# A gate by reciprocal, one product moved between engines, and a new order of all steps in a fused attention and channel-mixing kernel

## The chip, the cores and the metric

The kernel runs on one core of one Trainium2 chip. The metric is device time in microseconds (us), and of several runs the median. The core's engines work side by side and meet through semaphores: TensorE (PE in the profile) multiplies matrices and writes to PSUM, VectorE (DVE), ScalarE (ACT) and GpSimd (POOL) work elementwise, SyncE (SP) issues the DMA transfers here. Each engine takes its own instructions strictly in the order in which they stand.

## The reference

For four batches, attention of 12288 queries of width 128 over 768 keys, which are also the values; then a channel-mixing block on the attention's output.

```python
kv_pool = kv.reshape(B, H // r, r, W // r, r, C).mean(axis=(2, 4))
k = v = kv_pool.reshape(B, -1, C) @ w_sr
s = scale * (q @ k.transpose(0, 2, 1))
a = np.exp(s - s.max(-1, keepdims=True))
a /= a.sum(-1, keepdims=True) + 1e-09
x = a @ v

xk = mu_k * x + (1.0 - mu_k) * x_prev      # x_prev: x one position earlier
xr = mu_r * x + (1.0 - mu_r) * x_prev
k = np.maximum(xk @ w_k, 0.0)              # 128 -> 1024
v = k * k @ w_v                            # 1024 -> 128
r = 1.0 / (1.0 + np.exp(-(xr @ w_r)))      # the gate
out = r * v
```

All of it is float32, with inputs scaled so that the exponent of the gate can be large. The kernel keeps the accuracy by splitting operands of the fast matmuls into a high and a low part.

## The kernel before

A tile is 512 queries; there are 96 tiles, 24 per batch. Everything lies transposed, with the 128 channels on the partitions, except the scores.

The steps of a tile have short names, which the tables of times use; the profile shows the tile that a step writes.

- `qf` loads the queries, `qh` (ScalarE) and `ql` (GpSimd) split them.
- For each quarter s of the tile: `S` on TensorE gives 128x768 scores in PSUM; `nm` on VectorE their negated maximum; `ex` on ScalarE the exponentials (tile `pe`) and their sums. For two quarters at once `rc` on VectorE makes the scaled reciprocals of the sums, a TENSOR_SCALAR and a RECIPROCAL over 128x2. `f1` on ScalarE writes the high half of the weights (tile `pp`) and `f2` on VectorE the low half, from `pe` and the high half, both in SBUF. `tt` transposes them by DMA.
- `AV` on TensorE sums weights times values into `px` in PSUM. `xek` and `xer` (ScalarE), `xk` and `xr` (VectorE) mix it with the position before, and `xck`, `xcr` (GpSimd) copy the column that the next tile needs. `xkh` and `xrh` (VectorE) round to float16, and `xkl`, `xrl` (GpSimd) take the rest.
- For each quarter f of the 1024 hidden channels: `ha` and `hb` on TensorE give `ph`, 128x1024 in PSUM; `r` on ScalarE the positive part (tile `rr`). The square is needed as a float16 high part `kh` and a bfloat16 rest `kl`. A string with a figure per quarter says how: for "1" VectorE multiplies `ph` by `rr` (tile `kk`), ScalarE squares `rr` to float16 (`kh`) and GpSimd subtracts (`kl`); for "2" ScalarE squares to float32 (`kk`), VectorE casts it (`kh`) and GpSimd subtracts; for "3" VectorE multiplies in place in PSUM (profile: `ph<-ph,rr`) and also subtracts.
- `va` and `vb` on TensorE sum `kh` and `kl` times the second weights into `pv`.
- The gate: `z` on TensorE; `E` and `th` on ScalarE are the exponential and the hyperbolic tangent of half; `T1`, `E1` and `g` on VectorE make the gate of them, and `o` on VectorE multiplies `pv` by it. `so` stores `o`.

Keys of the next batch are made beside the tiles: twelve tiles of each of the first three batches hold one `br` (VectorE, TENSOR_REDUCE into `acc`), and later tiles the rest of that batch's preparation.

The order on every engine comes from tables of numbers. Each step of tile i gets the number `WHEN[step] + 19.3 * i` (the first and the last tiles have tables of their own, `EARLY` and `LATE`, the preparation `PREP` and `ONCE`), a heap hands the steps out by it, and a wrapper keeps each engine's instructions in that order:

```python
plan.add(places[name] + base, name, fn, ("tile", i))
while self.heap:
    heapq.heappop(self.heap)[2]()
```

Through the wrapper nearly every instruction is recorded under line 37, so the profile is read by tiles. PSUM holds three buffers of 128x1024, taken in turn by `S` and `ph`, one of 128x512 for `px` and the gate's `pz`, and one for `pv`.

Of the kernel before, what the change touches and what calls it, by code (L numbers as in the profile page):

```python
# [23 lines left out]
K_SHIFT = 23  # L24
# [47 lines left out]
def tile_kernel(ctx, tc, qT, kv0, kvw, w_sr, mu_k, mu_r, w_k, w_v, w_r, outT):  # L72
# [35 lines left out]
    cz = const.tile([P, 2], F32, name="cz")  # L108
# [3 lines left out]
    for name, shape, dtype in (  # L112
# [5 lines left out]
        ("E", [P, T], F32), ("th", [P, T], F32), ("o", [P, T], F32),  # L118
# [3 lines left out]
        ("s4", [P, 4], F32), ("uz", [P, 2], F32), ("sc", [P, 1], F32),  # L122
# [48 lines left out]
    def weights(name, w, hi, lo, half, extra):  # L171
# [6 lines left out]
        def part(i, c0, c1):  # L178
# [29 lines left out]
            @once(f"wi_{key}")  # L208
            def _():
                st["ei", i] = take("th", name="ei", dtype=I32)[:, :d]  # L210
                dve.tensor_scalar(
                    st["ei", i], st["ef", i], least, 2.0 ** 23, op0=ALU.subtract, op1=ALU.mult
                )
# [89 lines left out]
    @once("cz")  # L303
    def _():
        amp = one("amp_wr")
        unit = 1.0 / (scale * X_TOP)
        dve.tensor_scalar_mul(cz[:, 0:1], amp, unit)
        dve.tensor_scalar_mul(cz[:, 1:2], amp, 0.5 * unit)

    @once("cv")  # L310
    def _():
        unit = 1.0 / (scale * X_TOP)
        k2 = one("k2")
        dve.tensor_scalar(
            k2, one("amp_wk"), one("amp_wk"), 0.5 * unit * unit * 2.0 ** (2 * K_SHIFT),
            op0=ALU.mult, op1=ALU.mult,
        )
        dve.tensor_tensor(out=cv, in0=k2, in1=one("amp_wv"), op=ALU.mult)
# [187 lines left out]
    def plan_tile(i, b, t):  # L506
# [35 lines left out]
        for s in range(NSUB):  # L542
# [18 lines left out]
            @at(f"ex{s}")  # L561
            def _(s=s):
                if f"sm{s & 2}" not in st:
                    new(f"sm{s & 2}")
                act.activation(
                    out=new(f"pe{s}"), in_=st[f"S{s}"][:, :K], func=AF.Exp,
                    bias=st[f"nm{s}"], scale=1.0, accum_out=st[f"sm{s & 2}"][:, s % 2:s % 2 + 1],
                )
# [51 lines left out]
        for x, k in (("k", 0), ("r", 2)):  # L620
# [23 lines left out]
            def _(x=x):  # L644
                dve.tensor_copy(out=new(f"x{x}h"), in_=st[f"x{x}"])
# [15 lines left out]
        def _():  # L661
            act.activation(out=new("E"), in_=st["pz"], func=AF.Exp, scale=bps[b][5][:, 0:1])

        @at("th")
        def _():
            act.activation(out=new("th"), in_=st["pz"], func=AF.Tanh, scale=bps[b][5][:, 1:2])

        @at("T1")
        def _():
            th = st["th"].bitcast(I32)  # L670
            dve.tensor_single_scalar(th, th, 0x7FFFFFFF, op=ALU.bitwise_and)

        @at("E1")
        def _():
            dve.tensor_scalar(st["E"], st["E"], 1.0, bps[b][6], op0=ALU.min, op1=ALU.mult)

        @at("g")
        def _():
            dve.scalar_tensor_tensor(
                out=st["E"], in0=st["th"], scalar=1.0, in1=st["E"], op0=ALU.add, op1=ALU.mult  # L680
            )
# [76 lines left out]
        def _():  # L758
            dve.tensor_tensor(out=new("o"), in0=st["pv"], in1=st["E"], op=ALU.mult)
# [12 lines left out]
    for i, (b, t) in enumerate(seq):  # L772
# [8 lines left out]
KV = '1123'  # L781
# [12 lines left out]
    "xer": 88.618, "xcr": 88.633, "xck": 89.308, "xk": 89.863, "xkh": 91.073, "xr": 91.42,  # L794
# [14 lines left out]
    "ksl": 103.908,  # L809
# [38 lines left out]
        "xek": 112.355, "xer": 112.393, "xk": 112.842, "xcr": 113.081, "xr": 113.28, "xrh": 114.174,  # L848
# [222 lines left out]
```

## Time and profile before

| | |
|---|---|
| median of 3 runs | 2064.28 us (2064.04 to 2065.26) |
| the profiled execution | 2064.17 us, its span 2062.3 us |
| granted TensorE clock | 0.992 |
| busy, share of the span: PE, PEld, DVE, ACT, POOL | 93%, 51%, 96%, 83%, 56% |
| HBM read and written | 52.63 MB, 25.17 MB |

A row of the timeline gives start, duration, engine, operation, tile written and tiles read, shapes, and in brackets how long the engine was idle before and for whom. An instruction on VectorE starts some 0.07 us before the recorded end of the one ahead, so costs are best read from one start to the next. A row that groups instructions gives minimum, median and maximum in ns, or the summed time in us and the mean in ns. A row of a window gives its bounds, its length, the busy time of PE, PEld, DVE, ACT and POOL with the number of instructions, the granted clock, the share of DMA time and GB/s.

### The profile page before, as it was taken

To read this page: it belongs to the slowest core of one execution; us is meant where nothing else is said; L and a number is where in the kernel's file an instruction comes from. 1 tells how busy PE (TensorE), PEld (TensorE's weight loads), DVE (VectorE), ACT (ScalarE), POOL (GpSimd) and SP (SyncE) were. 2 spreads that over 40 slices of the span, in tenths; PEclk is the share of its full clock that TensorE was granted. 3 is DMA by queue.
4 is the path that set the end of the run, shared out by engine and by line. 5 is a ranking of instruction groups with operands and counts; after the bars stand their busy time and mean duration, and the time that the engine had idled before them with its cause. 6 is when DMAs were issued, how large, how long until landed. Compare 5 with 4: busy or idle time off the path is not lost. (4 is left out here: it accounts for less than half of the span.)

```text
span 2062.3 us, 26955 instructions
## 1 busy us (share of the span) xinstructions
PE 1911.9 (93%) x9022; PEld 1043.0 (51%) x9022; DVE 1987.1 (96%) x2581; ACT 1705.2 (83%) x2432; POOL 1155.9 (56%) x784
## 2 busy tenths in 40 slices
PE   6698999999999999999999999998999999999998
PEld 4344455554555555555555555554555555555553
DVE  6999999999999999999999999999999999999998
ACT  3687888888888888888888888887888888888896
POOL 1255565555555656556555656655565565555556
PEclk9899999999999999999999999999999999999999
DMA  7545455464656564644546565545445546455552
GB/s 218 125 96 132 108 126 100 91 115 82 124 112 142 114 140 106 118 88 100 105 105 140 111 145 111 125 84 111 93 106 99 117 89 123 89 116 106 104 101 58
DMA packets 640521, 230.56 MB, mean 112 GB/s; under 512 B 606336, under 2 KB 608640, under 8 KB 640384
## 3 DMA queue, kind: packets, MB, share of 16 engines
q1 hardware_dynamic: 640384, 228.85, 52.7%
q8 instruction: 71, 1.16, 0.3%
q14 instruction: 66, 0.54, 0.1%
HBM read 52.63 MB, written 25.17 MB: 38 GB/s over the span
## 5 line engine op out<-in xcount | busy, mean ns | idle before, releaser
L37 POOL TENSOR_TENSOR kl<-kk,kh 128x1024 bf16<-128x1024 f32 x288 | 688.0, 2390 | 478.3 <-ACT kh L37 230.2
L37 DVE SCALAR_TENSOR_TENSOR pp<-pe,rc,pp 128x768 f16<-128x768 f32 x384 | 552.2, 1474 | 0.1
L37 ACT ACTIVATE pe<-S,nm 128x768 f32<-128x768 f32 x384 | 346.2, 902 | 243.7 <-DVE nm L37 243.0
L37 ACT ACTIVATE rr<-ph 128x1024 f32<-128x1024 f32 x384 | 390.7, 1018 | 18.1 <-PE ph L37 14.4
L37 PE MATMUL px<-pT,v 128*128 128x512 f16 x1728 | 391.3, 379 | 2.8 <-DVE xr L37 2.3
L37 DVE TENSOR_REDUCE nm<-S 128x1 f32<-128x768 f32 x384 | 362.4, 945 | 3.8 <-PE S L37 3.4
L37 ACT ACTIVATE pp<-pe,rc 128x768 f16<-128x768 f32 x384 | 347.9, 932 | 7.9 <-DVE rc L37 2.6
L37 PE MATMUL S<-ksh,ql 128*128 128x512 f32 (+1 forms) x768 | 320.7, 418 | 34.7 <-DVE kk L37 20.0
L37 ACT ACTIVATE kh<-rr 128x1024 f16<-128x1024 f32 x288 | 303.1, 1053 | 0.5
L37 PE MATMUL ph<-xkh,wkl 128*128 128x512 f16 x768 | 293.4, 382 | 3.9 <-DVE kl L37 1.6
L37 PE MATMUL pv<-kh,wvl 128*128 128x512 f16 x768 | 293.3, 382 | 1.8 <-DVE kh L37 1.1
L37 PE MATMUL pv<-kh,wvh 128*128 128x512 f16 x768 | 292.0, 380 | 0.0
L37 PE MATMUL ph<-xkh,wkh 128*128 128x512 f16 x768 | 291.5, 380 | 0.0
L37 PEld LDWEIGHTS <-v 128*128 128x128 f16 x1728 | 168.6, 98 | 205.3 <-issue 3.0
L37 PE MATMUL S<-ksl,qh 128*128 128x512 f32 (+1 forms) x768 | 261.7, 341 | 0.4 <-DVE ksl L37 0.4
L37 PE MATMUL S<-ksh,qh 128*128 128x512 f32 (+1 forms) x768 | 261.1, 340 | 0.0
L37 POOL TENSOR_TENSOR ql<-qf,qh 128x512 fp32r<-128x512 f32 x96 | 123.8, 1289 | 206.7 <-ACT qh L37 206.7
L37 DVE TENSOR_TENSOR kk<-ph,rr 128x1024 f32<-128x1024 f32 x192 | 232.8, 1213 | 3.4 <-ACT rr L37 2.0
L37 PEld LDWEIGHTS <-wkh 128*128 128x128 f16 x1536 | 150.8, 98 | 165.0 <-issue 5.1
L37 PE MATMUL ph<-xkl,wkh 128*128 128x512 f16 x768 | 227.9, 379 | 0.0
L37 PE MATMUL pv<-kl,wvb 128*128 128x512 bf16 x768 | 227.3, 379 | 0.2 <-DVE kl L37 0.2
L37 PEld LDWEIGHTS S<-ksh,ql 128*128 128x128 f32 x768 | 146.4, 191 | 98.0 <-DVE kk L37 25.9
(116 smaller groups left out, 2651.6 us busy)
## 6 DMA issues: line engine op xcount, KB each, us to landing
qf<-qT SPq DMA_DIRECT2D x96, 256.0 KB, 3.3
outT<-o SPq DMA_DIRECT2D x96, 256.0 KB, 3.8
kvt<-kvw SPq DMA_DIRECT2D x36, 512.0 KB, 4.5
pT<-pp SPq DMA_TRANSPOSE x384, 4.1
kva<-kv SPq DMA_DIRECT2D x8, 512.0 KB, 5.5
kvb<-kv SPq DMA_DIRECT2D x4, 512.0 KB, 7.4
raw<-moe_w_k SPq DMA_DIRECT2D x2, 512.0 KB, 7.9
raw<-moe_w_v SPq DMA_DIRECT2D x2, 512.0 KB, 4.1
```

Of the source, the lines that this page charges most:

```text
L37: return self.tc.keep_in_program_order(op(*args, **kwargs))
```

## The change

- The gate becomes `E` (the exponential, now of minus z), `D` (VectorE: the smaller of E and 2^126, plus 1) and `g` (VectorE: RECIPROCAL in place over 128x512). `th` and `T1` go. The factor that `E1` multiplied in moves to `o`, which becomes a SCALAR_TENSOR_TENSOR.
- The third quarter of the hidden channels changes from "2" to "1": its product goes from ScalarE to VectorE, its rounding from VectorE to ScalarE.
- Two switches are added (where `pe` lies, and which engine makes `xkh`, `xrh` and `D`) and left as they were: SBUF and VectorE.
- All tables of numbers are new, and so is the order on every engine.

The core of the diff; of the tables only a line each is shown:

```diff
+                if PE_AT[s] == "P":
+                    st[f"pe{s}"] = st[f"S{s}"][:, :K]
+                else:
+                    new(f"pe{s}")
...
         @at("E")
         def _():
-            act.activation(out=new("E"), in_=st["pz"], func=AF.Exp, scale=bps[b][5][:, 0:1])
-
-        @at("th")
-        def _():
-            act.activation(out=new("th"), in_=st["pz"], func=AF.Tanh, scale=bps[b][5][:, 1:2])
-
-        @at("T1")
-        def _():
-            th = st["th"].bitcast(I32)
-            dve.tensor_single_scalar(th, th, 0x7FFFFFFF, op=ALU.bitwise_and)
-
-        @at("E1")
-        def _():
-            dve.tensor_scalar(st["E"], st["E"], 1.0, bps[b][6], op0=ALU.min, op1=ALU.mult)
+            act.activation(out=new("E"), in_=st["pz"], func=AF.Exp, scale=bps[b][5])
+
+        @at("D")
+        def _():
+            if CAST["D"] == "A":
+                act.activation(out=st["E"], in_=st["E"], func=AF.Copy, bias=1.0)
+            else:
+                dve.tensor_scalar(st["E"], st["E"], 2.0 ** 126, 1.0, op0=ALU.min, op1=ALU.add)
 
         @at("g")
         def _():
-            dve.scalar_tensor_tensor(
-                out=st["E"], in0=st["th"], scalar=1.0, in1=st["E"], op0=ALU.add, op1=ALU.mult
-            )
+            dve.reciprocal(st["E"], st["E"])
...
         @at("o")
         def _():
-            dve.tensor_tensor(out=new("o"), in0=st["pv"], in1=st["E"], op=ALU.mult)
+            dve.scalar_tensor_tensor(
+                out=new("o"), in0=st["pv"], scalar=bps[b][6], in1=st["E"], op0=ALU.mult, op1=ALU.mult
+            )
...
-KV = '1123'
+PE_AT = 'SSSS'
+CAST = {'k': 'D', 'r': 'D', 'D': 'D'}
+KV = '1113'
...
 WHEN = {
-    "br": 1.952, "qf": 14.922, "qh": 25.48, "ql": 28.691, "S0": 48.421, "S1": 49.355, "nm0": 49.552,
+    "br": 2.435, "qf": 13.848, "qh": 17.857, "ql": 24.148, "S0": 42.876, "nm0": 46.617,
...
```

What the tables move, at three places of an ordinary tile in the middle of the run. First VectorE around the gate, before, from the second `rc` of a tile on (`th` is `T1`, the two `E` are `E1` and `g`):

```order
L37 TENSOR_SCALAR rc<-sm 128x2
L37 RECIPROCAL rc<-rc 128x2
L37 CAST xrh<-xr 128x512
L37 TENSOR_SCALAR th<-th 128x512
L37 TENSOR_REDUCE nm<-S 128x1
L37 TENSOR_SCALAR E<-E,sc 128x512
L37 SCALAR_TENSOR_TENSOR E<-th,E 128x512
L37 TENSOR_TENSOR o<-pv,E 128x512
L37 TENSOR_TENSOR kk<-ph,rr 128x1024
```

and now (the TENSOR_SCALAR on `E` is `D`, the RECIPROCAL on `E` is `g`):

```order
L37 TENSOR_SCALAR rc<-sm 128x2
L37 RECIPROCAL rc<-rc 128x2
L37 TENSOR_REDUCE nm<-S 128x1
L37 CAST xrh<-xr 128x512
L37 SCALAR_TENSOR_TENSOR pp<-pe,rc,pp 128x768
L37 TENSOR_SCALAR E<-E 128x512
L37 TENSOR_REDUCE nm<-S 128x1
L37 RECIPROCAL E<-E 128x512
L37 SCALAR_TENSOR_TENSOR pp<-pe,rc,pp 128x768
```

The four `pp` steps of a tile no longer stand as two pairs: two of them stand singly on both sides of the gate. Then VectorE from the first `rc` behind this on, before:

```order
L37 TENSOR_SCALAR rc<-sm 128x2
L37 RECIPROCAL rc<-rc 128x2
L37 SCALAR_TENSOR_TENSOR pp<-pe,rc,pp 128x768 x2
L37 TENSOR_TENSOR kk<-ph,rr 128x1024
L37 SCALAR_TENSOR_TENSOR pp<-pe,rc,pp 128x768 x2
L37 TENSOR_REDUCE nm<-S 128x1
L37 SCALAR_TENSOR_TENSOR xk<-px,s_90,xek 128x512
L37 CAST xkh<-xk 128x512
L37 SCALAR_TENSOR_TENSOR xr<-px,s_90,xer 128x512
```

and now:

```order
L37 TENSOR_SCALAR rc<-sm 128x2
L37 RECIPROCAL rc<-rc 128x2
L37 SCALAR_TENSOR_TENSOR o<-pv,sc,E 128x512
L37 TENSOR_TENSOR kk<-ph,rr 128x1024
L37 SCALAR_TENSOR_TENSOR pp<-pe,rc,pp 128x768 x2
L37 SCALAR_TENSOR_TENSOR xr<-px,s_90,xer 128x512
L37 SCALAR_TENSOR_TENSOR xk<-px,s_90,xek 128x512
L37 TENSOR_TENSOR kk<-ph,rr 128x1024
L37 TENSOR_REDUCE nm<-S 128x1
L37 CAST xkh<-xk 128x512
```

One pair of `pp` is left, behind `o` and a product, and with four PSUM readers behind it; a `br`, in a tile that has one, stands between `o` and the product. The last place is GpSimd, one tile's worth before:

```order
L37 TENSOR_TENSOR ql<-qf,qh 128x512
L37 TENSOR_TENSOR kl<-kk,kh 128x1024
L37 COPY xer<-xer 128x1
L37 COPY xek<-xek 128x1
L37 TENSOR_TENSOR kl<-kk,kh 128x1024
L37 TENSOR_TENSOR xkl<-xk,xkh 128x512
L37 TENSOR_TENSOR kl<-kk,kh 128x1024
L37 TENSOR_TENSOR xrl<-xr,xrh 128x512
```

and now:

```order
L37 TENSOR_TENSOR ql<-qf,qh 128x512
L37 TENSOR_TENSOR kl<-kk,kh 128x1024 x2
L37 COPY xer<-xer 128x1
L37 TENSOR_TENSOR xkl<-xk,xkh 128x512
L37 TENSOR_TENSOR kl<-kk,kh 128x1024
L37 COPY xek<-xek 128x1
L37 TENSOR_TENSOR xrl<-xr,xrh 128x512
```

The first two `kl` of a tile now stand back to back behind `ql`, and the copies apart.

More of the change, by code (lines that the diff above doesn't have):

```diff
@@ L107, in tile_kernel @@
     mtop = const.tile([P, 2], F32, name="mtop")
-    cz = const.tile([P, 2], F32, name="cz")
+    cz = const.tile([P, 1], F32, name="cz")
     cv = const.tile([P, 1], F32, name="cv")
@@ L117, in tile_kernel @@
         ("xkh", [P, T], F16), ("xkl", [P, T], F16), ("xrh", [P, T], F16), ("xrl", [P, T], F16),
-        ("E", [P, T], F32), ("th", [P, T], F32), ("o", [P, T], F32),
+        ("E", [P, T], F32), ("ei", [P, T], F32), ("o", [P, T], F32),
         ("rr", [P, 2 * T], F32), ("kk", [P, 2 * T], F32), ("kh", [P, 2 * T], F16),
@@ L121, in tile_kernel @@
         ("ksh", [P, K], F32R), ("ksl", [P, K], F32R), ("v1", [P, NK, P], F16), ("v2", [P, NK, P], F16),
-        ("s4", [P, 4], F32), ("uz", [P, 2], F32), ("sc", [P, 1], F32),
+        ("s4", [P, 4], F32), ("uz", [P, 1], F32), ("sc", [P, 1], F32),
         ("ks", [P, K], F32), ("acc", [P, K], F32), ("dg", [P, 2, P], F32),
@@ L209, in _ @@
             def _():
-                st["ei", i] = take("th", name="ei", dtype=I32)[:, :d]
+                st["ei", i] = take("ei", dtype=I32)[:, :d]
                 dve.tensor_scalar(
@@ L306, in _ @@
         unit = 1.0 / (scale * X_TOP)
-        dve.tensor_scalar_mul(cz[:, 0:1], amp, unit)
-        dve.tensor_scalar_mul(cz[:, 1:2], amp, 0.5 * unit)
+        dve.tensor_scalar_mul(cz, amp, -unit)
     @once("cv")
@@ L314, in _ @@
         dve.tensor_scalar(
-            k2, one("amp_wk"), one("amp_wk"), 0.5 * unit * unit * 2.0 ** (2 * K_SHIFT),
+            k2, one("amp_wk"), one("amp_wk"), unit * unit * 2.0 ** (2 * K_SHIFT),
             op0=ALU.mult, op1=ALU.mult,
@@ L564, in _ @@
                     new(f"sm{s & 2}")
+                if PE_AT[s] == "P":
+                    st[f"pe{s}"] = st[f"S{s}"][:, :K]
+                else:
+                    new(f"pe{s}")
                 act.activation(
-                    out=new(f"pe{s}"), in_=st[f"S{s}"][:, :K], func=AF.Exp,
+                    out=st[f"pe{s}"], in_=st[f"S{s}"][:, :K], func=AF.Exp,
                     bias=st[f"nm{s}"], scale=1.0, accum_out=st[f"sm{s & 2}"][:, s % 2:s % 2 + 1],
@@ L644, in _ @@
             def _(x=x):
-                dve.tensor_copy(out=new(f"x{x}h"), in_=st[f"x{x}"])
+                if CAST[x] == "A":
+                    act.copy(out=new(f"x{x}h"), in_=st[f"x{x}"])
+                else:
+                    dve.tensor_copy(out=new(f"x{x}h"), in_=st[f"x{x}"])
             @at(f"x{x}l")
@@ L661, in _ @@
         def _():
-            act.activation(out=new("E"), in_=st["pz"], func=AF.Exp, scale=bps[b][5][:, 0:1])
-        @at("th")
+            act.activation(out=new("E"), in_=st["pz"], func=AF.Exp, scale=bps[b][5])
+        @at("D")
         def _():
-            act.activation(out=new("th"), in_=st["pz"], func=AF.Tanh, scale=bps[b][5][:, 1:2])
-        @at("T1")
-        def _():
-            th = st["th"].bitcast(I32)
-            dve.tensor_single_scalar(th, th, 0x7FFFFFFF, op=ALU.bitwise_and)
-        @at("E1")
-        def _():
-            dve.tensor_scalar(st["E"], st["E"], 1.0, bps[b][6], op0=ALU.min, op1=ALU.mult)
+            if CAST["D"] == "A":
+                act.activation(out=st["E"], in_=st["E"], func=AF.Copy, bias=1.0)
+            else:
+                dve.tensor_scalar(st["E"], st["E"], 2.0 ** 126, 1.0, op0=ALU.min, op1=ALU.add)
         @at("g")
         def _():
-            dve.scalar_tensor_tensor(
-                out=st["E"], in0=st["th"], scalar=1.0, in1=st["E"], op0=ALU.add, op1=ALU.mult
-            )
+            dve.reciprocal(st["E"], st["E"])
         for f in range(NF // 2):
@@ L787 @@
 WHEN = {
[6 rows of a table removed]
-    "xer": 88.618, "xcr": 88.633, "xck": 89.308, "xk": 89.863, "xkh": 91.073, "xr": 91.42,
[8 rows of a table removed]
[14 rows of a table added]
 }
 PREP = {
[3 rows of a table removed]
-    "ksl": 103.908,
[3 rows of a table added]
+    "ksl": 76.523,
 }
 ONCE = {
[25 rows of a table removed]
[25 rows of a table added]
 }
@@ L841 @@
     {
[6 rows of a table removed]
-        "xek": 112.355, "xer": 112.393, "xk": 112.842, "xcr": 113.081, "xr": 113.28, "xrh": 114.174,
[8 rows of a table removed]
-    },
-    {
[15 rows of a table removed]
-    },
-    {
[6 rows of a table removed]
-        "xck": 132.326, "xek": 132.734, "xer": 132.736, "xr": 135.63, "xk": 135.852, "xkh": 137.769,
[8 rows of a table removed]
-    },
-    {
[15 rows of a table removed]
-    },
-    {
[15 rows of a table removed]
-    },
-    {
[6 rows of a table removed]
-        "xer": 188.646, "xek": 189.257, "xcr": 191.216, "xr": 191.544, "xk": 192.408, "xkh": 194.637,
[8 rows of a table removed]
[6 rows of a table added]
+        "xek": 97.77, "xk": 97.792, "xkh": 97.992, "xer": 98.478, "xcr": 99.422, "xr": 100.482,
[7 rows of a table added]
+    },
+    {
[14 rows of a table added]
+    },
+    {
[6 rows of a table added]
+        "xcr": 124.51, "xer": 125.107, "xek": 127.181, "xr": 127.78, "xk": 129.317, "xkh": 130.977,
[7 rows of a table added]
+    },
+    {
[14 rows of a table added]
+    },
+    {
[14 rows of a table added]
+    },
+    {
[14 rows of a table added]
     },
@@ L946 @@
     {
[15 rows of a table removed]
-    },
-    {
[15 rows of a table removed]
-    },
-    {
[6 rows of a table removed]
-        "xer": 105.99, "xek": 107.611, "xk": 107.796, "xkh": 111.121, "xcr": 111.958, "xkl": 112.112,
[8 rows of a table removed]
-    },
-    {
[15 rows of a table removed]
[14 rows of a table added]
+    },
+    {
[14 rows of a table added]
+    },
+    {
[14 rows of a table added]
+    },
+    {
[6 rows of a table added]
+        "xer": 93.265, "xcr": 95.398, "xr": 95.62, "xck": 96.543, "xk": 97.359, "xkh": 99.68,
[7 rows of a table added]
     },
```

365 rows, old and new, of tables (EARLY, LATE, ONCE, PREP) are left out of this document.

## Prediction

> **What bounds the kernel now.** I read the page's totals, then the busy times of single tiles, then VectorE (DVE) and GpSimd (POOL) instruction by instruction over one tile, since two engines are nearly full.
>
> ```profile
> PE 1911.9 (93%) x9022; PEld 1043.0 (51%) x9022; DVE 1987.1 (96%) x2581; ACT 1705.2 (83%) x2432; POOL 1155.9 (56%) x784
> ```
>
> Next the busy time of each engine in two tiles, measured from one `o` on VectorE to the next. The first tile also sums keys for the next batch (a TENSOR_REDUCE named acc); the second has nothing beside its own work.
>
> ```profile
> 733.43:754.18 20.75, 19.58 (x95) 10.68 (x93) 20.52 (x27) 17.65 (x27) 12.45 (x8) 1.00 0.59 107
> 1575.09:1595.19 20.10, 19.29 (x94) 10.63 (x93) 19.52 (x26) 17.49 (x27) 10.70 (x8) 1.00 0.52 106
> L37 DVE TENSOR_REDUCE acc<-kvt x36: 1197/1199/1214, 66.3 to 1317.8; 128x64 f32<-128x1024 f32 x36
> ```
>
> So 36 tiles take 20.75 us and an ordinary one 20.10. TensorE (PE) needs 19.29 us of that: about 19.3 is the floor that this order of matmuls leaves. VectorE is busy for 19.52, but is it working? Its instructions in the second tile, in order of time:
>
> ```profile
> 1575.09 1.22 DVE L37 TENSOR_TENSOR kk<-ph,rr 128x1024 f32<-128x1024 f32 x1
> 1576.22 0.30 DVE L37 TENSOR_SCALAR rc<-sm 128x2 f32<-128x2 f32 x1
> 1576.56 0.17 DVE L37 RECIPROCAL rc<-rc 128x2 f32<-128x2 f32 x1
> 1576.64 3.80 DVE L37 SCALAR_TENSOR_TENSOR pp<-pe,rc,pp 128x768 f16<-128x768 f32 x2
> 1580.36 1.21 DVE L37 TENSOR_TENSOR kk<-ph,rr 128x1024 f32<-128x1024 f32 x1
> 1581.50 1.93 DVE L37 SCALAR_TENSOR_TENSOR pp<-pe,rc,pp 128x768 f16<-128x768 f32 x2
> 1583.35 0.95 DVE L37 TENSOR_REDUCE nm<-S 128x1 f32<-128x768 f32 x1
> 1584.22 0.74 DVE L37 SCALAR_TENSOR_TENSOR xk<-px,s,xek 128x512 f32<-128x512 f32 x1
> 1584.99 0.71 DVE L37 CAST xkh<-xk 128x512 f16<-128x512 f32 x1
> 1585.62 0.74 DVE L37 SCALAR_TENSOR_TENSOR xr<-px,s,xer 128x512 f32<-128x512 f32 x1
> 1586.29 0.94 DVE L37 TENSOR_REDUCE nm<-S 128x1 f32<-128x768 f32 x1
> 1587.15 1.22 DVE L37 TENSOR_TENSOR ph<-ph,rr 128x1024 f32<-128x1024 f32 x1
> 1588.28 0.68 DVE L37 CAST kh<-kk 128x1024 f16<-128x1024 f32 x1
> 1588.88 1.21 DVE L37 TENSOR_TENSOR kl<-ph,kh 128x1024 bf16<-128x1024 f32 x1
> 1590.01 0.94 DVE L37 TENSOR_REDUCE nm<-S 128x1 f32<-128x768 f32 x1
> 1590.88 0.38 DVE L37 TENSOR_SCALAR rc<-sm 128x2 f32<-128x2 f32 x1
> 1591.29 0.17 DVE L37 RECIPROCAL rc<-rc 128x2 f32<-128x2 f32 x1
> 1591.38 0.41 DVE L37 CAST xrh<-xr 128x512 f16<-128x512 f32 x1
> 1591.70 0.42 DVE L37 TENSOR_SCALAR th<-th 128x512 int32<-128x512 int32 x1
> 1592.03 0.95 DVE L37 TENSOR_REDUCE nm<-S 128x1 f32<-128x768 f32 x1
> 1592.90 0.52 DVE L37 TENSOR_SCALAR E<-E,sc 128x512 f32<-128x512 f32 x1
> 1593.45 0.69 DVE L37 SCALAR_TENSOR_TENSOR E<-th,E 128x512 f32<-128x512 f32 x1
> 1594.59 0.69 DVE L37 TENSOR_TENSOR o<-pv,E 128x512 f32<-128x512 f32 x1 [0.44 <-PE pv L37]
> ```
>
> And GpSimd's in the same stretch:
>
> ```profile
> 1575.21 1.29 POOL L37 TENSOR_TENSOR ql<-qf,qh 128x512 fp32r<-128x512 f32 x1 [2.19 <-ACT qh L37]
> 1576.99 2.63 POOL L37 TENSOR_TENSOR kl<-kk,kh 128x1024 bf16<-128x1024 f32 x1 [0.49 <-ACT kh L37]
> 1583.28 2.14 POOL L37 TENSOR_TENSOR kl<-kk,kh 128x1024 bf16<-128x1024 f32 x1 [3.58 <-ACT kh L37]
> 1585.78 1.16 POOL L37 TENSOR_TENSOR xkl<-xk,xkh 128x512 f16<-128x512 f32 x1 [0.36 <-DVE xkh L37]
> 1589.10 2.13 POOL L37 TENSOR_TENSOR kl<-kk,kh 128x1024 bf16<-128x1024 f32 x1 [2.16 <-DVE kh L37]
> 1591.86 1.27 POOL L37 TENSOR_TENSOR xrl<-xr,xrh 128x512 f16<-128x512 f32 x1 [0.63 <-DVE xrh L37]
> ```
>
> The pair of pp steps costs 3.72 us from start to next start at 1576.64, and 1.85 at 1581.50. In the first case a kl of GpSimd came in 0.35 after the first pp step, got its turn after it and ahead of the second: 1.87 us lost. The steps that suffer so read two SBUF operands (pp) or are single-source SBUF steps (rc, xkh); steps with a PSUM operand (kk, nm, xk) run through. I call the first kind excluding steps. Taking starts to next starts, VectorE's undisturbed work is: four nm at 0.87 = 3.48; four pp at 0.925 = 3.70; kk, kk, ph, kl at 1.13 = 4.52; two rc pairs at 0.27 (0.42 less what 0.30 is above the minimum 0.15, quoted below) = 0.54; xk 0.77; xr 0.67; two casts at 0.32 = 0.64; kh 0.60; th 0.33; E 0.45 and 0.60; o 0.60. Sum 16.90. The other 3.2 of 20.10 are 1.87 at pp, 0.32 at xkh, 0.15 at each rc, 0.10 at E, 0.44 for pv, and trifles. VectorE bounds the kernel, but by waits for GpSimd, not by work.
>
> **The change, part by part, per tile.** *Product for cast:* kk at 1.13 instead of kh at 0.60: +0.53. ScalarE swaps one 128x1024 step for another. *Gate:* out go th 0.33, E 0.45 and 0.60, and o at 0.60 (1.98). In come D, of th's kind (0.33), o with a scalar (0.67, as xr), and a reciprocal over 512 elements, R. ScalarE loses its Tanh; it isn't the bound. *Order:* xk is no longer followed directly by the cast that reads it: 0.67 for 0.77.
>
> R is nowhere in the trace at this size. What there is:
>
> ```profile
> L37 DVE TENSOR_SCALAR rc<-sm x192: 148/332/1120, 34.1 to 2015.7; 128x2 f32<-128x2 f32 x192
> L37 DVE RECIPROCAL rc<-rc x192: 165/166/169, 34.3 to 2016.9; 128x2 f32<-128x2 f32 x192
> L37 DVE RECIPROCAL ivs<-exs 128x1 f32<-128x1 f32 x4 | 0.7, 164 | 0.1
> ```
>
> The TENSOR_SCALAR spreads from 148 to 1120 ns, the RECIPROCAL next to it never moves: it seems not to be an excluding step, so it runs one element at a time. Then a second element costs 2 ns, and 512 at most 164 + 511x2 = 1190 ns. From below, th's 0.33. I take 0.60, as o: one element at a time, 512 of them. Then the gate is 0.33 + 0.60 + 0.67 = 1.60, saving 0.38, and the work is 16.90 + 0.53 - 0.38 - 0.10 = 16.95: no saving at all. What decides is where GpSimd's steps fall now.
>
> I lay the new order out from the start of xrh, t = 0. pp starts at 0.32 and ends its turn at 1.25; GpSimd's xrl asks at 0.48 (1591.38 to 1591.86), so D, asking at 1.25, waits for it: a GpSimd step in between costs its length less 0.27 (2.14 gave 1.87), here 1.00. Queued behind D on VectorE are nm, the reciprocal and a pp, and ScalarE's next pe waits for that nm. nm and the reciprocal follow, during which ql may run; it waits for qh, and I take 0.25 for the part that delays the next pp (0 to 0.5). xkl and the last kl, 1.16 + 2.14 from 0.49 after xkh starts, run beside ph, nm and kl (3.13), and the rc behind them waits 0.2. Sum 1.45, so VectorE needs 18.4: less than TensorE's 19.3. An ordinary tile takes 19.3: -0.8.
>
> One place is tight: after the second rc pair (end T) VectorE does o, kk, pp, pp, and GpSimd's second kl must not fall between the two pp. It waits for ScalarE: two pp and a kh from T on.
>
> ```profile
> 1577.72 1.76 ACT L37 ACTIVATE pp<-pe,rc 128x768 f16<-128x768 f32 x2
> 1579.37 1.02 ACT L37 ACTIVATE rr<-ph 128x1024 f32<-128x1024 f32 x1
> 1582.14 1.05 ACT L37 ACTIVATE kh<-rr 128x1024 f16<-128x1024 f32 x1
> ```
>
> 1.65 + 1.05 and 0.2 for handing over: T + 2.9. The second pp asks at T + 0.67 + 1.13 + 0.925 = T + 2.7. It wins by 0.2. In the 36 tiles with acc, that step (1.12) stands before the kk: the pp ask at T + 2.9 and T + 3.85, kl gets in between, and pays 1.87. Such a tile needs 18.4 + 1.12 + 1.87 = 21.4: +0.65.
>
> The rest of the reordering I cost at nothing. DMA issues move on SP's queue, transposes and loads earlier, the store later, but the DMA engines are busy for 0.52 to 0.59 of these tiles and nothing in the second tile waits for one. The stretch before the first `o` and the tail after the last are reordered too; I keep their lengths:
>
> ```profile
> L37 DVE TENSOR_TENSOR o<-pv,E x96: 671/692/693, 116.7 to 2058.7; 128x512 f32<-128x512 f32 x96
> ```
>
> Sum over the 95 intervals in between: 36 x 0.65 = +23; the other 59 at -0.8 = -47 (tiles with a batch's preparation counted alike). The profiled execution took 2064.17 around a span of 2062.3, the runs' median is 2064.28: **2040 us**. R's ends move it only in the 36 tiles, by -0.27 to +0.59 each: 2030 to 2061. With 10 us for the start and half a ql delay more or less per tile, the case's own range is 1995 to 2080.
>
> **Rivals.**
>
> *The kl misses the gap in the acc tiles too*, because ScalarE's kh comes 0.9 later than I put it. Those tiles then need 18.4 + 1.12 = 19.5: 36 x -1.25 = -45, in all 1972. For it: ScalarE is busy 17.5 of 20.1. Against: it sits waiting for rc at that place.
>
> *The kl hits the gap in every tile.* My margin is 0.2 us. Then an ordinary tile needs 18.4 + 1.87 = 20.3, +0.2: 12 + 23 gives about 2099, slower. It decides once kl asks before T + 2.7.
>
> [...]
>
> **How the numbers follow.** Forecast 0.41, kl missing the gap 0.22, kl always in the gap 0.14, the slow reciprocal 0.18, and 0.05 for no change, waits only changing place. Time 2040; the range 1955 to 2112 takes in all but the slow reciprocal and some ends. A change under 0.2% (4 us) can't be told from none here. Faster: 0.22 and 0.35 of the forecast's 0.41, 0.57; same 0.06; slower 0.37.
>
> **What would show it.** RECIPROCAL E at 0.6 to 0.7 us, and no longer when GpSimd is busy. TENSOR_SCALAR E (D) about 1 us longer than its 0.42. Intervals between `o` of 19.3 in ordinary and 21.4 in acc tiles; pp means still far above 1005 ns in the acc tiles, with kl between the pair. Wrong would be: RECIPROCAL over 1.2 us, acc tiles under 20.75, or ordinary tiles over 20.1.

## The result, and the profile after

The changed kernel takes 2234.23 us (median of 4 runs, 2233.01 to 2235.55) where the kernel before takes 2064.23 (2064.04 to 2065.26): a ratio of 1.0823, 95% interval 1.0804 to 1.0841. It is slower by 170 us, where the prediction had 2040 us. The profiled execution took 2234.37 us around a span of 2232.6.

From the page of the changed kernel: the totals, and two groups of instructions (busy us and mean ns, then idle time before them).

```profile
PE 1978.7 (89%) x9022; PEld 1048.5 (47%) x9022; DVE 2164.5 (97%) x2484; ACT 1657.0 (74%) x2336; POOL 1151.1 (52%) x784
L37 DVE SCALAR_TENSOR_TENSOR pp<-pe,rc,pp 128x768 f16<-128x768 f32 x384 | 461.3, 1220 | 0.2 <-ACT pp L37 0.2
L37 DVE RECIPROCAL E<-E 128x512 f32<-128x512 f32 x96 | 320.4, 3337 | 0.1
```

VectorE is the full engine still, and the long RECIPROCAL takes 320 us of it: 3.34 us each, where the prediction's sum had 0.60. The pp are shorter than before (1220 ns for the 1474 that before's page has), so waits did go.

Busy time by engine between two `o`, first in a tile with acc, then in an ordinary one:

```profile
864.77:888.42 23.65, 19.96 (x95) 10.59 (x93) 23.58 (x26) 17.16 (x24) 12.26 (x9) 1.00 0.48 111
1926.88:1947.96 21.08, 19.93 (x94) 10.59 (x93) 20.77 (x26) 16.94 (x24) 11.72 (x9) 1.00 0.51 101
```

They were 20.75 and 20.10 before: +2.90 and +0.98. VectorE in the ordinary tile, at the places that the prediction spoke of:

```profile
1928.68 2.05 DVE L37 SCALAR_TENSOR_TENSOR pp<-pe,rc,pp 128x768 f16<-128x768 f32 x2
...
1940.28 1.39 DVE L37 TENSOR_SCALAR E<-E 128x512 f32<-128x512 f32 x1
1941.59 0.94 DVE L37 TENSOR_REDUCE nm<-S 128x1 f32<-128x768 f32 x1
1942.46 3.33 DVE L37 RECIPROCAL E<-E 128x512 f32<-128x512 f32 x1
1945.72 0.91 DVE L37 SCALAR_TENSOR_TENSOR pp<-pe,rc,pp 128x768 f16<-128x768 f32 x1
```

GpSimd in the same stretch:

```profile
1929.79 2.94 POOL L37 TENSOR_TENSOR kl<-kk,kh 128x1024 bf16<-128x1024 f32 x1 [0.80 <-ACT kh L37]
...
1939.52 1.86 POOL L37 TENSOR_TENSOR xrl<-xr,xrh 128x512 f16<-128x512 f32 x1 [1.37 <-DVE xrh L37]
1942.47 1.27 POOL L37 TENSOR_TENSOR ql<-qf,qh 128x512 fp32r<-128x512 f32 x1 [1.09 <-ACT qh L37]
```

The pair of pp runs undisturbed, since kl asks 1.11 us after its start, when the second, 0.93 after the first, has asked already. D waits behind xrl: 1940.28 to 1941.59 is 1.31, 0.98 above the 0.33 of its kind. And ql runs from 1942.47 on beside the RECIPROCAL and takes 1.27 (1.29 before), while the RECIPROCAL's own length hardly differs over the 96 tiles (minimum, median and maximum in ns):

```profile
L37 DVE RECIPROCAL E<-E x96: 3334/3336/3353, 112.4 to 2225.5; 128x512 f32<-128x512 f32 x96
```

So it is no excluding step. From its start to the next start it takes 3.26 us. In the tile with acc, VectorE and then GpSimd:

```profile
865.43 1.21 DVE L37 TENSOR_REDUCE acc<-kvt 128x64 f32<-128x1024 f32 x1
866.56 1.21 DVE L37 TENSOR_TENSOR kk<-ph,rr 128x1024 f32<-128x1024 f32 x1
867.69 3.81 DVE L37 SCALAR_TENSOR_TENSOR pp<-pe,rc,pp 128x768 f16<-128x768 f32 x2
```

```profile
867.95 2.74 POOL L37 TENSOR_TENSOR kl<-kk,kh 128x1024 bf16<-128x1024 f32 x1 [1.08 <-DVE kk L37]
```

The kl comes 0.26 after the first pp has started and ahead of the second: the pair takes 3.74 (867.69 to 871.43, where the next step starts) for 1.85, the collision that the prediction laid out. Its moment is another: the kl waits for the kk here and comes 3.18 after the prediction's T, the start of `o` at 864.77, where the prediction had T + 2.9 from ScalarE's kh.

### The profile page after: what moved, and what is told of

Same layout as the page of the kernel before. It is cut to its first block, busy times and chain, and to the rows that moved or that the text cites. A ratio compares the mean times of both kernels' runs of the same rounds, so it can differ in the third digit from the quotient of the medians.

```text
span 2232.6 us, 27116 instructions
## 1 busy us (share of the span) xinstructions
PE 1978.7 (89%) x9022; PEld 1048.5 (47%) x9022; DVE 2164.5 (97%) x2484; ACT 1657.0 (74%) x2336; POOL 1151.1 (52%) x784
## 5 line engine op out<-in xcount | busy, mean ns | idle before, releaser
L37 POOL TENSOR_TENSOR kl<-kk,kh 128x1024 bf16<-128x1024 f32 x288 | 679.0, 2358 | 502.8 <-DVE rc L37 349.8
L37 DVE SCALAR_TENSOR_TENSOR pp<-pe,rc,pp 128x768 f16<-128x768 f32 x384 | 461.3, 1220 | 0.2 <-ACT pp L37 0.2
L37 PE MATMUL px<-pT,v 128*128 128x512 f16 x1728 | 407.5, 380 | 0.6 <-DVE mx_wr L37 0.6
L37 ACT ACTIVATE kh<-rr 128x1024 f16<-128x1024 f32 x384 | 393.9, 1054 | 0.9
L37 ACT ACTIVATE rr<-ph 128x1024 f32<-128x1024 f32 x384 | 381.0, 1016 | 10.3 <-PE ph L37 7.7
L37 DVE TENSOR_TENSOR kk<-ph,rr 128x1024 f32<-128x1024 f32 x288 | 349.2, 1212 | 6.9 <-ACT rr L37 4.0
L37 DVE RECIPROCAL E<-E 128x512 f32<-128x512 f32 x96 | 320.4, 3337 | 0.1
L37 PE MATMUL pv<-kh,wvl 128*128 128x512 f16 x768 | 300.0, 391 | 11.4 <-DVE o L37 9.1
L37 POOL TENSOR_TENSOR xrl<-xr,xrh 128x512 f16<-128x512 f32 x96 | 172.1, 1793 | 139.3 <-DVE xrh L37 139.2
L37 POOL TENSOR_TENSOR xkl<-xk,xkh 128x512 f16<-128x512 f32 x96 | 112.2, 1169 | 254.5 <-DVE xkh L37 248.3
```

The lines of the kernel that those rows point to most:

```text
L37: return self.tc.keep_in_program_order(op(*args, **kwargs))
```

## The experiments

Theory: the order, its waits and the collision are as the prediction laid them out, and one number was wrong, the reciprocal's. Rival: the new order costs time by itself. Each ratio below is to runs of the kernel before that were taken beside the run, with medians from 2063.13 to 2064.97.

### 1. The reciprocal by itself

```diff
+    for n in (1, 2, 3, 4, 8, 16, 32, 64, 96, 128, 192, 256, 384, 512, 768):
+        for _ in range(4):
+            dve.reciprocal(rs[:, 0:n], rs[:, 0:n])
...
```

> The kernel before, with RECIPROCALs in place over scratch added on VectorE behind the last o: four each over 128x1, 2, 3, 4, 8, 16, 32, 64, 96, 128, 192, 256, 384, 512 and 768 float32 elements, four from PSUM, and three while GpSimd is at work. Theory A (a fixed price per element, hidden at one and two elements by a floor): from one start to the next 60 ns + 6.25 ns per element above a floor near 80 ns, so 160 at 16, 460 at 64, 860 at 128, 1660 at 256, 3260 at 512, 4860 at 768; the same from PSUM and beside GpSimd. Theory B (about 2 ns per element as the prediction read it, and the 3.26 us of 512 elements a property of this place in the kernel or of a long stream): 64 elements near 0.2 us, 128 near 0.35, and 512 well under 3 us or a jump at some length.

Groups of VectorE's instructions in this run:

```profile
L37 DVE RECIPROCAL rs<-rs 128x1 f32<-128x1 f32 x4 | 0.6, 151 | 0.1
L37 DVE RECIPROCAL rs<-rs 128x2 f32<-128x2 f32 x4 | 0.7, 166 | 0.1
L37 DVE RECIPROCAL rs<-rs 128x8 f32<-128x8 f32 x4 | 0.8, 204 | 0.1
L37 DVE RECIPROCAL rs<-rs 128x64 f32<-128x64 f32 x4 | 2.2, 553 | 0.1
L37 DVE RECIPROCAL rs<-rs 128x768 f32<-128x768 f32 x4 | 19.8, 4953 | 0.1
L37 DVE RECIPROCAL rt<-rq 128x512 f32<-128x512 f32 x4 | 13.4, 3357 | 0.1
```

From 8 to 768 elements the recorded length is 153 ns + 6.25 ns per element to within a nanosecond (153 + 50 = 203, 153 + 400 = 553, 153 + 4800 = 4953), and nearly the same from PSUM (rq: 3357 for 153 + 3200 = 3353). Even the step from one element to two is 15 ns here, not 2. Three of 512 elements, with GpSimd busy beside the first two and the start of the third, took no longer, 10.13 us for three times 3.35 (VectorE, then GpSimd):

```profile
2155.09 10.13 DVE L37 RECIPROCAL rs<-rs 128x512 f32<-128x512 f32 x3
```

```profile
2155.14 7.80 POOL L37 TENSOR_TENSOR rb<-rb 128x1024 f32<-128x1024 f32 x4 [96.16 <-DVE rb L37]
```

Theory A's price per element holds. Where did the prediction's 2 ns come from? It subtracted the mean of one instruction (ivs, one element) from that of another (rc, two). The profile of before holds a third row that would have warned:

```profile
L37 DVE RECIPROCAL xi<-xt 128x2 f32<-128x2 f32 x4 | 0.6, 152 | 0.0
```

Two elements at 152 ns, fewer than ivs' 164 for one: rows of different instructions differ by more than the slope that was read from them.

### 2. The changed kernel with a short reciprocal

```diff
-            dve.reciprocal(st["E"], st["E"])
+            dve.reciprocal(st["E"][:, 0:88], st["E"][:, 0:88])
```

> The changed kernel with its long RECIPROCAL cut to the first 88 of 512 columns, so that it takes the 0.6 us that the prediction gave it; the gate of the other columns is left as 1+exp(-z). Theory A (order and waits as laid out, only the size of the reciprocal was wrong): ordinary tiles 19.3 us, tiles with acc 21.4, in all 2040 us (1995 to 2080). Theory B (the new order costs by itself): more than 2090 us, ordinary tiles over 20.1.

Measured: 2026.74 us, ratio 0.9822 (0.9806 to 0.9838). The tile with acc and the ordinary one:

```profile
791.83:813.42 21.59, 19.57 (x93) 10.57 (x94) 21.52 (x27) 17.27 (x24) 12.28 (x9) 1.00 0.55 122
1750.92:1770.04 19.12, 19.07 (x93) 10.61 (x93) 18.79 (x25) 17.07 (x24) 11.72 (x9) 1.00 0.55 111
```

Forecast 21.4 and 19.3, measured 21.59 and 19.12, and TensorE is busy for 19.07 of the latter: with the price that the prediction gave the reciprocal, both kinds of tile come out within 0.2 us of its forecast. The rival falls, at this price. The second length:

```diff
-            dve.reciprocal(st["E"], st["E"])
+            dve.reciprocal(st["E"][:, 0:200], st["E"][:, 0:200])
```

> The changed kernel with its long RECIPROCAL cut to 200 of 512 columns, 1.31 us (the gate of the others is left as 1+exp(-z)): the point from which, by the prediction, the change begins to lose. Theory A (the layout with R as the only wrong size): 0.70 more than with 88 columns, of which GpSimd's ql, that then runs beside it, gives back some 0.5 at the next pp: ordinary tiles 19.2 to 19.5 us, tiles with acc 21.7 to 22.0, in all 2037 to 2065 us. Theory B (the loss goes straight with the reciprocal's length from the start): 2027 + 95 x 0.70 = 2093 us.

Measured: 2043.52 us, ratio 0.9898 (0.9883 to 0.9913). In the same order:

```profile
799.40:821.10 21.70, 19.52 (x92) 10.60 (x93) 21.63 (x27) 17.16 (x24) 12.26 (x9) 1.00 0.54 121
1763.24:1782.39 19.15, 19.10 (x94) 10.58 (x94) 18.84 (x25) 16.95 (x24) 11.74 (x9) 1.00 0.54 111
```

Theory A again: 0.70 us more of reciprocal costs 0.11 and 0.03 in such tiles (the rest of the 17 us lies in other ones), because the slack in front of TensorE (VectorE is busy for 18.79 of the ordinary tile's 19.12 with 88 columns) and the time for which ql had held up the next pp swallow it. That pp, in an ordinary tile with 88 columns:

```profile
1767.24 1.47 DVE L37 SCALAR_TENSOR_TENSOR pp<-pe,rc,pp 128x768 f16<-128x768 f32 x1
```

It has 0.91 in the changed kernel, where ql runs out beside the reciprocal: 0.56 of the 0.70. From here to 512 elements there is nothing left to swallow: 1.95 us more of reciprocal cost 1.95 and 1.93 in such tiles, and 190.7 us in all, about 95 x 2.0. A straight line between the two runs reaches before's 2064.2 at R = 1.5 us, an estimate, where by the prediction's sum the change begins to lose at 1.3 (0.67 over its 0.60 in each of 36 tiles is the 24 us from 2040 to 2064).

### 3. The parts of the change apart

The gate alone, in the order of before:

```diff
 # order and KV = '1123' of before; E, D, g, o, cz, cv of the change
+for places in [WHEN] + EARLY + LATE:
+    places["D"] = max(places.pop("E1"), places.pop("T1"))
+    places.pop("th")
```

> The kernel before in its own order, with the new gate alone: th and T1 gone, D at the later of T1's and E1's places, g as RECIPROCAL, o with the scalar. Theory A (the reciprocal carries the whole loss): 0.33 + 3.26 + 0.67 in place of 1.98, +2.28 per tile, less up to 0.44 that o waited for pv: tiles of 22.0 to 22.4 us, in all 2240 to 2281 us, so nothing is gained over the changed kernel. Theory B (a good part of the loss is the new order's): clearly under the changed kernel's 2234, 2150 or so.

Measured: 2383.08 us, ratio 1.155 (1.1533 to 1.1567), 100 us over the top of what theory A expected. An ordinary tile of this run, and VectorE in it:

```profile
2055.03:2078.87 23.84, 19.36 (x94) 10.67 (x94) 23.61 (x24) 16.94 (x25) 12.43 (x8) 1.00 0.51 89
```

```profile
2057.11 3.83 DVE L37 SCALAR_TENSOR_TENSOR pp<-pe,rc,pp 128x768 f16<-128x768 f32 x2
2060.86 1.21 DVE L37 TENSOR_TENSOR kk<-ph,rr 128x1024 f32<-128x1024 f32 x1
2061.99 3.81 DVE L37 SCALAR_TENSOR_TENSOR pp<-pe,rc,pp 128x768 f16<-128x768 f32 x2
```

GpSimd and ScalarE around the second pair:

```profile
2062.21 2.77 POOL L37 TENSOR_TENSOR kl<-kk,kh 128x1024 bf16<-128x1024 f32 x1 [1.23 <-DVE kk L37]
```

```profile
2057.28 1.76 ACT L37 ACTIVATE pp<-pe,rc 128x768 f16<-128x768 f32 x2 [1.08 <-issue]
...
2060.99 1.06 ACT L37 ACTIVATE kh<-rr 128x1024 f16<-128x1024 f32 x1
```

So both pairs of pp have a kl in between. Before, the second pair was safe because its kl waited for ScalarE's kh, which ended (1582.14 + 1.05) 2.83 after the start of the kk. A slower VectorE, as these rows read, leaves ScalarE ahead of its work: its two pp start 0.17 after VectorE's first, where they started 1.08 after it, and kh now ends 1.19 after the kk's start. So kh is done by the time that kk ends (2062.05 and 2062.07), and kl comes at 2062.21 and gets in. That is 1.88 per tile (3.81 less the 1.93 of before) on top of the gate's 2.3, and neither theory had it: the longer step on VectorE brought a wait of its own. (The tile is 3.74 longer and not 4.2, since 0.4 of the waits that xkh and the rc had before are gone.) It also shows what the new order, with the product, is worth when the reciprocal is in: 2383 to 2234.

The order and the product alone, with the old gate:

```diff
 # order and KV = '1113' of the change; E, th, T1, E1, g, o, cz, cv of before
+for places in [WHEN] + EARLY + LATE:
+    places["th"] = places["E"] + 0.0005
+    places["E1"] = places["D"]
+    places["T1"] = places.pop("D") + 0.0005
```

> The changed kernel's order and product with the old gate put back: th behind E on ScalarE, E1 and T1 at D's place, g at the reciprocal's, o without the scalar. Theory A: work 16.95 - 1.60 + 1.98 = 17.33, and g reads two SBUF operands and so may wait for ql, up to 1.0: ordinary tiles 19.3 to 19.8, tiles with acc 21.8 to 22.8, in all 2080 us (2045 to 2130). Theory B (the new order costs by itself): 2150 us or more.

Measured: 2082.79 us, ratio 1.0095 (1.008 to 1.011); the tile with acc and the ordinary one:

```profile
814.47:836.65 22.18, 19.69 (x93) 10.58 (x93) 22.11 (x27) 17.63 (x25) 12.27 (x9) 1.00 0.53 119
1798.52:1818.19 19.67, 19.57 (x94) 10.52 (x93) 19.36 (x26) 17.52 (x25) 11.72 (x9) 1.00 0.56 108
```

Theory A, at the middle of its range. So of the 170 us, 19 come with the order and the product, and 151 with the gate on top of them. The ordinary tiles gain (19.67 for 20.10), the tiles with acc lose more (22.18 for 20.75). The gate's own sum fits: g takes 1.42 here for its 0.60 (1814.44 to 1815.86), since it waits for ql (in another tile ql runs for 1.27 from 1774.77, and g, begun at 1775.09, gives way to the next step at 1776.51), and 19.67 + 2.28 - 0.82 is 21.13, where the changed kernel's ordinary tile takes 21.08.

The product alone, in the order of before:

```diff
-KV = '1123'
+KV = '1113'
+for places in [WHEN] + EARLY + LATE:
+    places["kh2"] = places["k22"]
+    places["k22"] = places["r2"] + 0.0005
```

> The kernel before with the third quarter's product on VectorE and its rounding on ScalarE alone; the product stands right behind the r of that quarter, since in the old cast's place it would wait for itself. Theory A (the product's price as in the prediction's sum, 1.13 for 0.60): +0.53 us per tile, ordinary tiles 20.66, in all 2114 us. Theory B (shifting the steps moves another kl of GpSimd between two pp or takes one away): 1.87 more or less per tile on top, near 2290 or 1940 us.

Measured: 2132.04 us, ratio 1.0326 (1.0309 to 1.0343). An ordinary tile, and the `o` of another:

```profile
1834.69:1855.66 20.97, 19.36 (x94) 10.68 (x93) 19.72 (x25) 17.53 (x27) 11.59 (x8) 1.00 0.48 101
```

```profile
1708.89 0.69 DVE L37 TENSOR_TENSOR o<-pv,E 128x512 f32<-128x512 f32 x1 [0.96 <-PE pv L37]
```

Between the theories, and near A: an ordinary tile is 0.87 longer for A's 0.53, with a longer wait of `o` for pv (0.96 for 0.44), and one with acc only 0.23 (20.98 for 20.75). The product had to stand elsewhere than the cast, so this is the price of product and place together; the two can't be told apart by this run.

### 4. The waits that the new order still has

The step into acc moved behind the pair of pp, one number in the table:

```diff
-    "br": 2.435, "qf": 13.848, ...
+    "br": 6.45, "qf": 13.848, ...
```

> The changed kernel with one number changed: br (the TENSOR_REDUCE into acc) moved from ahead of the kk to behind the pair of pp. Theory A (the kl gets between the pair in the tiles with acc because of that step): those 36 tiles lose the collision, 1.5 to 1.9 us each from 23.66, so 21.8 to 22.2, in all 2166 to 2180 us. Theory B (the collision only moves, or the 36 tiles are long for another reason, a transfer or the step itself): 2225 us or more.

Measured: 2184.6 us, ratio 1.0583 (1.0567 to 1.0599). A tile with acc:

```profile
844.86:866.75 21.89, 19.68 (x92) 10.58 (x93) 21.82 (x27) 17.05 (x24) 11.75 (x9) 1.00 0.52 120
```

21.89 for 23.65. The pair of pp in another such tile of this run:

```profile
780.98 2.05 DVE L37 SCALAR_TENSOR_TENSOR pp<-pe,rc,pp 128x768 f16<-128x768 f32 x2
```

It takes 2.05 for 3.81: the collision is gone, as theory A has it. The 49.6 us in all are less than 36 x 1.76 = 63, and the count is why. In the changed kernel, up to its seventh `o`:

```profile
L37 DVE TENSOR_REDUCE acc<-kvt x7: 1198/1199/1210, 86.4 to 222.8; 128x64 f32<-128x1024 f32 x7
```

Seven of the 36 steps fall in the first tiles, which have tables of their own; 29 x 1.76 = 51 is close to what was gained. The same move with the old gate, and then `xrh` one nm earlier as well:

```diff
-    "xkh": 86.731, ... "xrh": 93.547, ...
+    "xkh": 86.731, ... "xrh": 92.95, ...
```

> The changed kernel's order and product with the old gate, and br moved behind the pair of pp. Theory A: 2083 less 36 x 1.5 to 1.9, so 2015 to 2029 us, ordinary tiles as before at 19.68, faster than both kernels. Theory B (the collision only moves): 2075 us or more.

> As the run before, with xrh put one nm earlier on VectorE too, so that GpSimd's xrl is nearly done when E1 asks. Theory A: of the 1.0 us that E1 waits for xrl 0.6 to 0.9 goes; VectorE then needs some 18.9 in an ordinary tile and TensorE's 19.15 is the floor: 19.15 to 19.3, in all 1970 to 2010 us. Theory B (TensorE or ScalarE sets the 19.68 already): no change against the run before.

Measured: 2039.14 us, ratio 0.9876 (0.9862 to 0.9891), above its range. Most of that is the same wrong count: with 29 tiles the range is 2028 to 2039, and such a tile lost 1.70 (20.48 for 22.18). Then 1961.68 us, ratio 0.9499 (0.9483 to 0.9515), better than its range and faster than both kernels. The tile with acc and the ordinary one of the latter:

```profile
763.13:782.29 19.16, 19.05 (x92) 10.62 (x93) 18.89 (x28) 17.42 (x26) 11.46 (x9) 1.00 0.64 138
1682.03:1701.18 19.15, 19.10 (x93) 10.61 (x93) 17.84 (x26) 17.41 (x26) 11.43 (x9) 1.00 0.53 111
```

E1 (minimum, median and maximum in ns) in the run with the old gate alone, and here:

```profile
L37 DVE TENSOR_SCALAR E<-E,sc x96: 466/1383/1467, 99.1 to 2074.7; 128x512 f32<-128x512 f32 x96
```

```profile
L37 DVE TENSOR_SCALAR E<-E,sc x96: 466/475/1473, 99.3 to 1955.3; 128x512 f32<-128x512 f32 x96
```

The wait for xrl, 0.9 us of E1, is gone. So is one that the expectation had left out, that of g for ql: the median of g falls from 1494 to 675 ns. Both kinds of tile are at TensorE's 19.1, and VectorE has 1.3 us to spare in an ordinary one. Theory B (TensorE or ScalarE had set the 19.68) falls. With this kernel's third quarter changed back to the cast:

```diff
-KV = '1113'
+KV = '1123'
+for places in [WHEN] + EARLY + LATE:
+    if places["kh2"] < places["k22"]:
+        places["k22"], places["kh2"] = places["kh2"], places["k22"]
```

> The fastest kernel so far (new order, old gate, br and xrh moved) with the third quarter changed back, the product on ScalarE and the cast on VectorE. Theory A (TensorE sets 19.15 us of an ordinary tile, VectorE has 0.2 to 0.7 to spare): 1955 to 1975 us. Theory B (the cast reads and writes SBUF alone and waits for GpSimd, where the product with its PSUM operand does not): waits of 0.5 to 1.5 us at kh, over 1990 us.

Measured: 1975.9 us, ratio 0.9575 (0.9561 to 0.9589), 1 us over theory A's range. A tile with acc and an ordinary one:

```profile
767.94:787.47 19.53, 19.37 (x95) 10.66 (x94) 19.12 (x28) 17.52 (x26) 11.77 (x9) 1.00 0.67 135
1690.84:1709.98 19.14, 19.14 (x94) 10.59 (x93) 17.39 (x26) 17.41 (x26) 11.47 (x9) 1.00 0.53 111
```

Nothing in an ordinary tile, 0.37 in those with acc, where kh takes 1.36 for its 0.60 (775.77 to 777.13) and VectorE is busy for 19.12 where it was 18.89, with 0.53 less work, so that a wait as in theory B does show there. In this order the product on VectorE, with its place, is worth 14 us in all. Last, the new gate in that order, first with the numbers of br and xrh alone:

> The changed kernel with its full reciprocal, br behind the pair of pp and xrh one nm earlier: how far the order can make up for the reciprocal. Theory A (the work of VectorE with R = 3.26 is 16.95 + 2.66 = 19.6 us a tile, above TensorE's 19.15, so only waits can be saved): D no longer waits 1.0 for xrl, 0.6 to 0.9 per tile less than the run with br alone: ordinary tiles 20.2 to 20.5, tiles with acc 21.0 to 21.3, in all 2100 to 2128 us, still slower than before. Theory B (as in the runs with the old gate, where this move was worth 77 us in all): 2107 us or less, and tiles with acc at the ordinary tiles' length.

Then with `D` on ScalarE as well:

```diff
-CAST = {'k': 'D', 'r': 'D', 'D': 'D'}
+CAST = {'k': 'D', 'r': 'D', 'D': 'A'}
```

> As the run before, with D on ScalarE (1 + E without the upper bound of 2^126). Theory A (VectorE's sum bounds): 0.33 us and what is left of D's wait go, ScalarE has the room: 0.35 to 0.7 less per tile, 2040 to 2095 us. Theory B (ScalarE takes its steps in order, D stands behind others there, and the reciprocal then waits for it): no gain, or longer.

Measured: 2124.12 us, ratio 1.0292 (1.0276 to 1.0307), with 20.40 and 21.20 us per tile as theory A expected. Its sum fits: with this reciprocal VectorE's undisturbed work, 19.6, lies above TensorE's 19.15 already. And 2251.72 us, ratio 1.091 (1.0893 to 1.0926), with D on ScalarE. VectorE and ScalarE in that run:

```profile
1715.06 3.35 DVE L37 RECIPROCAL E<-E 128x512 f32<-128x512 f32 x1 [1.77 <-ACT E L37]
```

```profile
1712.98 1.01 ACT L37 ACTIVATE rr<-ph 128x1024 f32<-128x1024 f32 x1
1713.88 0.61 ACT L37 CAST qh<-qf 128x512 fp32r<-128x512 f32 x1
1714.39 0.63 ACT L37 ACTIVATE E<-E 128x512 f32<-128x512 f32 x1
```

Theory B: D stands behind rr and qh on ScalarE, and VectorE idles for it 1.77 us ahead of this reciprocal (151.7 us ahead of 88 of the 96), more than the 0.33 that D costs on VectorE undisturbed.

## Why the prediction was wrong

**The step that failed** is one term of its sum, "I take 0.60, as o: one element at a time, 512 of them", and the end above it, "512 at most 164 + 511x2 = 1190 ns". It measured 3.26, 2.66 more per tile. The reasoning ahead of it held in part: the RECIPROCAL is no excluding step. But that it isn't held up by GpSimd (165 to 169 ns over two elements before, 3334 to 3353 over 512 now) says nothing on its time per element, which is 6.25 ns, and the bound was a difference between two unlike rows (experiment 1). So an end called a bound was none, and the range, which left the slow reciprocal out, missed.

**The rival that was nearest** is the slow reciprocal, given 0.18 and left outside the range. No run had shown its length when that chance was put down; all that the traces had were 164 and 166 ns at one and two elements, read as 2 ns for the second. The runs show 3.26 us at 512 elements from its start to the next, and 6.25 ns per element in recorded length (experiment 1), about six times the 1.0 ns by which the prediction's own kk and nm differ (1.13 us for 1024 less 0.87 for 768 elements). Put the 2.66 more into the prediction's 18.4 and 21.4, give back the 0.25 that it took for ql, and ordinary tiles come to 20.8 and those with acc to 23.8; measured 21.08 and 23.65. Its chance was too low.

**Point by point otherwise.**

- Waits for GpSimd and not work bound the kernel before: right. The fastest run keeps the old gate, gives VectorE more work, the product, and is 5% faster.
- D comes 1.00 late behind xrl: 0.98 was measured.
- The collision in the tiles with acc costs 1.87: 1.89 was measured (3.74 less 1.85).
- The second pp asks ahead of kl in ordinary tiles: right, by 0.2 as said. The first pp starts at 1928.68, so the second asks 0.93 later, at 1929.61, and kl asks at 1929.79.
- TensorE's floor is 19.3: 0.2 too high (19.12, experiment 2).
- The reordering's remaining edits cost nothing, and the stretch before the first `o` and the tail keep their lengths: not quite. In the run with the short reciprocal the seventh `o` starts at 227.5 where it started at 235.0 before, a gain of 7.5 us that the sum doesn't have; the tail behind the last `o` is 3.6 us in both.
- ql delays a pp by 0.25: low, it was 0.56 (experiment 2).
- "36 tiles" should have been 29, which makes the forecast at 0.60 us 2030 instead of 2040. 2026.7 was measured. That it is so near is in part luck, since the errors named here go both ways.
- By the sum the change begins to lose with a reciprocal of 1.3 us: it was 1.5, by the estimate of experiment 2.

**Where the 170 us are.** 29 tiles at +2.90 make 84. The 60 others behind the seventh `o` make 59 if all of them are counted as ordinary, at +0.98. The first six intervals between `o` hold 11 more, at a granted clock of 0.96 where it was 1.00 before: the seventh `o` of the changed kernel starts at 245.8 and its first at 116.2, of before at 235.0 and 116.7:

```profile
L37 DVE SCALAR_TENSOR_TENSOR o<-pv,sc,E x7: 734/742/749, 116.2 to 245.8; 128x512 f32<-128x512 f32 x7
```

```profile
L37 DVE TENSOR_TENSOR o<-pv,E x7: 671/682/692, 116.7 to 235.0; 128x512 f32<-128x512 f32 x7
```

Of the 16 left over nearly 5 are in four of the 29 tiles, which take 24.80 to 24.82 at a granted TensorE clock of 0.93. One of them (the clock is the last figure but two):

```profile
888.42:913.24 24.82, 21.44 (x96) 11.38 (x94) 23.69 (x27) 17.27 (x24) 12.25 (x9) 0.93 0.46 86
```

The rest lies in the tiles with a batch's preparation, in the last ones and in a few others. Over the whole run the clock is 0.979, where it was 0.992 before. Why it is lower in the changed kernel no run here shows; in the two tiles that are compared above it is 1.00 in both kernels. The 29 comes from counting: seven of the 36 acc steps come ahead of the seventh `o`.

## What to carry to other kernels

A price read at one or two elements was mostly the instruction's fixed part here (the RECIPROCAL's 166 ns at two elements, of which two at 6.25 ns are 12.5), and a slope taken between rows of different instructions was noise (2 ns from ivs to rc, -12 ns from ivs to xi): where no row has the size, the honest upper end is the worst price per element that anything speaks for. Between VectorE and GpSimd, whose steps shut each other out at a pair of pp for 1.88 us, a longer step didn't only add its length, it also shifted which steps meet: the same gate cost 319 us in one order and 151 in another, which has the product too. And a pair of excluding steps was protected by what is put around it: two numbers in the table, for acc and xrh, were worth 121 us with the old gate (2082.8 to 1961.7), and turned a loss against the kernel before into a gain of 5%.

## What the runs showed of the hardware that was not expected

VectorE's RECIPROCAL costs 6.25 ns per element (153 ns + 6.25 ns per element from 8 to 768 elements, float32, in SBUF; 3357 ns for 512 from PSUM and 3353 from SBUF), and a GpSimd instruction beside it changed nothing (3334 to 3353 ns in all 96 tiles of the changed kernel, ql beside it in those shown), where the pp behind it, a step with two SBUF operands, waited 0.56 us for the same ql in the run with 88 columns. And VectorE, slowed by the reciprocal, met a step of GpSimd that only ScalarE's lateness had kept apart from it: ScalarE's kh, 1.6 us earlier against VectorE's kk, cost 1.88 us per tile in the run with the gate alone.
